# Where the third part of the hidden values is made: beside the first layer or beside the second

## The chip, the cores and the metric

The kernel runs on one core of a Trainium2 chip. The metric is the device time of one execution in microseconds (us). A core has TensorE (PE, matrix products; its weight loads are listed as PEld), VectorE (DVE), ScalarE (ACT), GpSimd (POOL) and SyncE (SP, which only starts transfers). Each engine works through its own instructions in program order and waits on semaphores for the others.

## The reference

Two blocks follow each other: a gated linear recurrence over 768 steps for 4 batches and 8 heads of 48 dimensions, and a mixture of four experts that every token goes through.

```python
for t in range(S):
    state = alpha[:, :, t, :, None] * state + np.einsum('bhd,bhe->bhde', k[:, :, t], v[:, :, t])
    y[:, :, t] = np.einsum('bhd,bhde->bhe', q[:, :, t], state)
x = y.transpose(0, 2, 1, 3).reshape(B * S, H * D)          # 3072 x 384
p = domain_probs / (domain_probs.sum(-1, keepdims=True) + 1e-09)
for e in range(E):                                         # 4 experts, F = 1024
    h = np.maximum(x @ w1[e], 0.0)
    out += p[:, e:e + 1] * (h @ w2[e])
```

All data is fp32. The change lies in the expert part alone, between `np.maximum` and `h @ w2[e]`.

## The kernel before

**Groups.** A block is 128 time steps of one batch; there are 24. They are taken in seven groups: group 0 has two blocks, groups 1 to 5 have four, group 6 has two. For each group and each expert there is a first layer (`up`, once for each of eight tiles of 128 hidden rows) and a second layer (`down`). Groups 5 and 6 alternate expert by expert at the end. While the experts of one group run, the attention of the next group's blocks is slipped in: `attention` is a generator, and `advance` runs its next stretch when a planned clock has reached the stretch's time (`deal`). The last group's attention is over before group 5 begins, so groups 5 and 6 have none beside them.

**Three parts.** TensorE multiplies most operands in a faster fp32 format[...]. To keep accuracy, operands are split in three parts that are stored one beside the other: top, low and "dif", called D here. The three products of parts (D with one part of the weights, top and low with the two others) are summed in two accumulators. From group 1 on the first layer runs in this way, from group 2 on the second layer too (`split1`, `split2`).

**First layer.** `up` takes three k-chunks of x and three parts: six products into the accumulator `one`, three into `two`, each 512 columns wide for a group of four blocks. ScalarE scales `one` into `t` (L551), VectorE adds `two` (L553). The rest, `hidden_parts`, is put off to the next tile so that it stands behind that tile's products: ScalarE makes top with a ReLU (L578), VectorE makes low (L580), and then comes D (`make_dif`, L590), one instruction for 256 columns, that is, for a pair of blocks. VectorE's order for a tile is therefore low and D of the tile before, then the add of this one.

For a group of four blocks the first 256 columns of D, those of the first pair of blocks, are made at once (L586), and the other 256 are put in the queue `later`. For group 6, with its 256 columns, all goes to `later`.

**Second layer.** `down` takes two blocks at a time (`slots`), so a group of four has a first pair and a second pair, each with 48 products of 384 columns (L624), numbered n from 0:

- 0 to 23: top, then low, of the hidden tiles 0 to 5 for both blocks
- 24 to 31: the same of tiles 6 and 7
- 32 to 39: D of tiles 0 to 7 for the pair's first block, 40 to 47 for its second block

At n = 3, 7, 11 and so on one entry is taken off `later` (L620). With eight entries, the last is made at n = 31. In a group of four blocks all eight are taken in the first pair's `down`, and they are D of the second pair.

**Sums.** A block has two accumulators in PSUM, one for top and low, one for D. When one is complete, `add_up` scales it by the expert's weight and adds it to `acc`: on VectorE (L658), but for the first expert on ScalarE where the accumulator is the first one (L656). The four PSUM buffers with the tag `g` serve `one`, `two` and the second layer's accumulators in turn, so the second pair's `down` can begin only when the first pair's first accumulator has been added up.

**Splits of x.** At the last expert of a group the next group's x is split in its three parts (`split_x`): the top parts on ScalarE at the start of the first pair, low and D on VectorE (L248, L249) in the first half of the second pair.

Of the kernel before, what the change touches and what calls it, by code (L numbers as in the profile page):

```python
# [20 lines left out]
def kernel(  # L21
# [41 lines left out]
    P = 128  # L63
# [7 lines left out]
    NT = B * P  # L71
# [11 lines left out]
    n = np.arange(QUAD)[None, :]  # L83
# [55 lines left out]
    splitting = []  # L139
    stores = deque()  # L140
    late = deque()
    later = deque()
    shared = {}
    accs = {}

# [41 lines left out]
    def load_piece(l, i, beside=False):  # L187
        if i >= E * NQ * LAST:
            return
        gi, k = divmod(i, E * NQ)  # L190
        e, c = divmod(k, NQ)
        if (split1, split2)[l](gi, e):
            w = wt[l][i] = wts.tile([P, 3, KC * QF], F32R, name=f"w{l + 1}",
                                    bufs=AHEAD if l == 0 else NQ)
            nc.sync.dma_start(out=w.bitcast(F32), in_=kept[l][k])
            return
        if l == 1 and not beside:
            return
        if l == 0:

            if gi > 0 or e == 0:
                shared[c] = wts.tile([P, 3, KC * QF], F32R, name="w2", bufs=NQ)
            w = shared[c][:, 2 - e % 2 if gi == 0 else 2].bitcast(F32)
        else:

            w = hidden[c][:, 0].rearrange("p f n -> p (f n)")[:, :KC * QF].bitcast(F32)
        wt[l][i] = w
        if l == 0:
            heads = moe_w1[e].rearrange("(h d) f -> h d f", d=D)[:, :, c * QF:(c + 1) * QF]
            w = w.rearrange("p (c f) -> p c f", f=QF)  # L210
            for part in range(2):
                nc.sync.dma_start(out=w[:, part], in_=heads[part * H // 2:(part + 1) * H // 2, :QUAD])
            nc.sync.dma_start(out=w[:, 2], in_=heads[:, QUAD:])
        else:
            nc.sync.dma_start(
                out=w.rearrange("p (c d) -> p c d", d=DM),
                in_=moe_w2[e].rearrange("(c p) d -> p c d", p=P)[:, c * FPQ:(c + 1) * FPQ])

    def split_piece(l, i):
        whole = wt[l][i]  # L220
        w = wts.tile([P, 3, KC * QF], F32R, name=f"w{l + 1}", bufs=AHEAD if l == 0 else NQ)
        top, low, dif = (w[:, part] for part in range(3))

        nc.scalar.activation(out=top, in_=whole, func=ACT.Copy, scale=TRIM)
        yield
        nc.scalar.activation(out=dif, in_=whole, func=ACT.Copy, scale=TRIM * 4096)
        yield
        nc.vector.scalar_tensor_tensor(out=low, in0=whole, scalar=4096.0, in1=dif.bitcast(F32),
                                       op0=ALU.mult, op1=ALU.subtract)
        nc.vector.tensor_sub(dif, low.bitcast(F32), top.bitcast(F32))  # L230
        nc.gpsimd.dma_start(out=kept[l][i % (E * NQ)], in_=w.bitcast(F32))
        if l == 0:
            del wt[0][i]

    def background():


        for piece in list(splitting):
            if next(piece, splitting) is splitting:
                splitting.remove(piece)  # L240
        if making and len(splitting) < 4:
            splitting.append(making.popleft())
            next(splitting[-1])
# [332 lines left out]
    def hidden_parts(x, parts):  # L576
        top, low, dif = parts
        nc.scalar.activation(out=top, in_=x, func=ACT.Relu, scale=TRIM)  # L578
        yield
        nc.vector.scalar_tensor_tensor(out=low, in0=x, scalar=0.0, in1=top.bitcast(F32),  # L580
                                       op0=ALU.max, op1=ALU.subtract)

        n = x.shape[-1]
        at = n // 2 if n == NT else 0
        if at:
            make_dif(*(part[:, :at] for part in parts))  # L586
        later.append([part[:, at:] for part in parts])

    def make_dif(top, low, dif):
        nc.vector.scalar_tensor_tensor(out=dif, in0=top.bitcast(F32), scalar=1 / 4096.0,  # L590
                                       in1=low.bitcast(F32), op0=ALU.mult, op1=ALU.subtract)
# [5 lines left out]
    def down(gi, e, slots, between):  # L597


        first = first_piece(gi, e)  # L600
        halves_ = split2(gi, e)
        if slots[0] == 0 and makes[1](gi, e):
            making.extend(split_piece(1, first + k) for k in range(NQ))
        if slots[0] == 0 and makes[0](gi, e) and 0 < e < E - 1:
            making.extend(split_piece(0, first + k) for k in range(2, NQ))
        sums = [[ps.tile([P, DM], F32, name=f"ops{j}", tag="g", bufs=4)
                 for j in range(2 if halves_ else 1)] for _ in slots]

        kinds = [((0, 1), range(FCH - 2)), ((0, 1), range(FCH - 2, FCH)), ((2,), range(FCH))]
        steps = [(part, i, fc) for parts, tiles in (kinds if halves_ else [((3,), range(FCH))])  # L610
                 for part in parts for i in range(len(slots)) for fc in tiles]
        for n, (part, i, fc) in enumerate(steps):
            c, f = divmod(fc, FPQ)
            h = hidden[c][:, :, f, slots[i] * P:(slots[i] + 1) * P]
            advance(cost(1, gi, e) / FCH / (3 if halves_ else 1))
            while between and n >= between[0][0] * len(steps):
                between.popleft()[1]()
            if n == len(steps) // 2:
                background()
            if later and n % 4 == 3:  # L620
                make_dif(*later.popleft())
            if halves_:
                w = wt[1][first + c].rearrange("p t (c d) -> p t c d", d=DM)[:, part, f]
                nc.tensor.matmul(sums[i][part // 2], lhsT=h[:, part], rhs=w,  # L624
                                 start=(fc == 0 and part != 1), stop=(fc == FCH - 1 and part != 0))
            else:
                w = wt[1][first + c].rearrange("p (c d) -> p c d", d=DM)[:, f]
                nc.tensor.matmul(sums[i][0], lhsT=h[:, 2].bitcast(F32), rhs=w,  # L628
                                 start=(fc == 0), stop=(fc == FCH - 1))
            if part >= 1 and fc == FCH - 1:  # L630
                add_up(gi, e, slots[i], part // 2, sums[i][part // 2 if halves_ else 0])
        while between:
            between.popleft()[1]()
        background()
        if slots[-1] == len(groups[gi]) - 1 and gi != LAST - 1:
            while makes[1](gi, e) and (making or splitting):
                background()

            for c in range(NQ):
                del wt[1][first + c]  # L640
                if c < NQ // 2 or gi == LAST:
                    load_piece(1, first + NQ + c)
                else:
                    late.append(first + NQ + c)

    def add_up(gi, e, slot, kind, part):

        cb, b = groups[gi][slot]
        at = b * NCB + cb
        if e == 0 and (kind == 0 or not split2(gi, e)):  # L650
            accs[cb, b] = hid.tile([P, DM], F32, name="acc", bufs=B) if gi < LAST else \
                work.tile([P, NP * P], F32, name="QT")[:, :DM]
        acc = accs[cb, b]
        scale = (p_fine if kind == 0 else p_all)[:, at, e:e + 1]
        if e == 0 and (kind == 0 or not split2(gi, e)):
            nc.scalar.activation(out=acc, in_=part, func=ACT.Copy, scale=scale)  # L656
        else:
            nc.vector.scalar_tensor_tensor(out=acc, in0=part, scalar=scale, in1=acc,  # L658
                                           op0=ALU.mult, op1=ALU.add)
        if kind == 0:  # L660
            return
        if e == E - 1:
            del accs[cb, b]
            row = b * S + cb * P
            stores.append(lambda: (nc.sync if gi >= LAST - 1 else nc.gpsimd).dma_start(
                out=out[row:row + P, :], in_=acc))
# [3 lines left out]
    def cost(layer, gi, e):  # L670
        n = len(groups[gi]) / 4
        if layer == 0:
            return 2.1 * n if split1(gi, e) else 2.6 * n
        return 4.1 if split2(gi, e) else 5.4
# [32 lines left out]
    def advance(spent):  # L707
        nonlocal clock
        clock += spent
        while waiting and clock >= waiting[0][0]:  # L710
            next(waiting.popleft()[2], None)

    with tc.manual_schedule():
# [48 lines left out]
        for (gi, e), after in zip(tasks, [*tasks[1:], (None, None)]):  # L762
# [6 lines left out]
            for k, slots in enumerate(turns):  # L769

                between = deque()
                if after[1] == 0:
                    for step, at in enumerate((0.0, 0.52, 0.62, 0.72)):
                        at = at * len(turns) - k
# [33 lines left out]
```

## Time and profile before

| | before |
|---|---|
| time, median of 3 runs | 1072.71 us (1072.09 to 1073.56) |
| span of the profiled execution | 1071.6 us |
| TensorE products busy | 1048.1 us, 98% |
| TensorE weight loads busy | 899.1 us, 84% |
| VectorE busy | 775.2 us, 72% |
| ScalarE busy | 566.7 us, 53% |
| D on VectorE (L590) | 288 instructions, 111.9 us |

The whole span is TensorE's: its products are marked busy 98% of the time. Products are pipelined and their recorded ends are modelled, so a short wait can lie under a "busy" row. The distance from one product's start to the next says more, and so does the list of what the weight loads waited for. In the rows of the timeline the first number is the start in us, the second the length of the row, then engine, line of the program, operation, what it writes and reads, shapes, and how many instructions are merged in the row; in brackets is the idle time before it and what ended it. In the lists of waits the numbers are the total in us, how many waits, and the longest. In the groups of instructions, the numbers after the count are busy us in all, mean ns of one, and idle us before them.

### The profile page before, as it was taken

To read this page: it belongs to the slowest core of one execution; us is meant where nothing else is said; L and a number is where in the kernel's file an instruction comes from. 1 tells how busy PE (TensorE), PEld (TensorE's weight loads), DVE (VectorE), ACT (ScalarE), POOL (GpSimd) and SP (SyncE) were. 2 spreads that over 40 slices of the span, in tenths; PEclk is the share of its full clock that TensorE was granted. 3 is DMA by queue.
4 is the path that set the end of the run, shared out by engine and by line. 5 is a ranking of instruction groups with operands and counts; after the bars stand their busy time and mean duration, and the time that the engine had idled before them with its cause. 6 is when DMAs were issued, how large, how long until landed. Compare 5 with 4: busy or idle time off the path is not lost.

```text
span 1071.6 us, 21614 instructions
## 1 busy us (share of the span) xinstructions
PE 1048.1 (98%) x8460; PEld 899.1 (84%) x8460; DVE 775.2 (72%) x1711; ACT 566.7 (53%) x1202; POOL 32.7 (3%) x71
## 2 busy tenths in 40 slices
PE   8899999999999999999999999999999999999998
PEld 8777777676776798898898898898889889898988
DVE  5488776656566978778877777986787866666565
ACT  5687866575656554536546445555464543323232
POOL 2010000000000100000000000000000000000000
PEclk9999999999999999999999999999999999999999
DMA  8597699687696967758759558586594543544540
GB/s 123 156 330 216 230 328 368 238 328 241 236 309 209 402 216 274 281 160 312 268 170 359 204 187 337 186 281 234 158 358 173 221 192 147 207 177 178 187 181 31
DMA packets 158838, 251.67 MB, mean 235 GB/s; under 512 B 120112, under 2 KB 135344, under 8 KB 136208
## 3 DMA queue, kind: packets, MB, share of 16 engines
q1 hardware_dynamic: 149600, 208.82, 57.1%
q0 software_dynamic: 5760, 41.29, 9.8%
q8 instruction: 67, 1.10, 0.4%
q10 hardware_dynamic: 3376, 0.17, 0.3%
q14 instruction: 35, 0.29, 0.1%
HBM read 207.79 MB, written 42.47 MB: 234 GB/s over the span
## 4 chain that ended last, share of the span: by engine, by line
PE 83%; DVE 8%; ACT 6%; issue 2%; DMA 1%; SPq 0%; DVEq 0%; ACTq 0%
PE ops L624 25%; PE one L540 21%; PE ops L628 10%; PE two L540 10%; PE sc L334 6%; PE yps L428 3%; PE tp L266 3%; PE one L532 2%; ACT qb L308 2%; PE far L389 1%; PE sps L463 1%; DVE near L344 1%; DVE t L553 1%; DVE hT L580 1%; DVE hT L590 1%
## 5 line engine op out<-in xcount | busy, mean ns | idle before, releaser
L624 PE MATMUL ops<-w,hT 128*128 128x384 f32 x1728 | 318.0, 339 | 4.4 <-DVE acc L658 4.3
L624 PEld LDWEIGHTS ops<-w,hT 128*128 128x128 f32 x1728 | 299.1, 188 | 9.9 <-DVE acc L658 5.6
L540 PE MATMUL one<-xT,w 128*128 128x512 f32 x960 | 253.8, 400 | 2.6 <-DVE xT L248 1.1
L540 PEld LDWEIGHTS one<-xT,w 128*128 128x128 f32 x960 | 176.3, 188 | 41.8 <-DVE QT L315 1.6
L551 ACT ACTIVATE t<-one 128x512 f32<-128x512 f32 (+1 forms) x192 | 106.3, 554 | 153.6 <-PE one L540 148.5
L308 ACT COPY qb<-QT 64x256 f32<-64x256 f32 x336 | 136.4, 406 | 77.0 <-DVE QT L289 44.1
L578 ACT ACTIVATE hT<-t 128x512 fp32r<-128x512 f32 (+1 forms) x160 | 94.3, 589 | 123.6 <-DVE t L553 122.9
L580 DVE SCALAR_TENSOR_TENSOR hT<-t,hT 128x512 fp32r<-128x512 f32 (+1 forms) x160 | 102.2, 638 | 55.7 <-ACT hT L578 53.6
L540 PE MATMUL two<-xT,w 128*128 128x512 f32 x480 | 136.7, 393 | 0.0
L628 PE MATMUL ops<-hT 128*128 128x384 f32 x384 | 133.4, 491 | 0.0
L553 DVE TENSOR_TENSOR t<-t,two 128x512 f32<-128x512 f32 (+1 forms) x160 | 100.8, 630 | 41.9 <-ACT t L551 21.4
L590 DVE SCALAR_TENSOR_TENSOR hT<-hT 128x256 fp32r<-128x256 f32 x288 | 111.9, 422 | 4.4
L540 PEld LDWEIGHTS two<-xT,w 128*128 128x128 f32 x480 | 90.6, 189 | 20.0
L628 PEld LDWEIGHTS ops<-hT 128*128 128x128 f32 x384 | 69.5, 190 | 40.1 <-issue 0.4
L315 DVE TENSOR_TENSOR QT<-QT,dec 128x256 f32<-128x256 f32 x144 | 60.8, 422 | 38.2 <-ACT qb L308 37.5
L344 DVE COPY_PREDICATED near<-masks,sc 128x256 f32<-128x256 uint8 x144 | 77.0, 535 | 15.5 <-PE sc L334 12.8
L334 PEld LDWEIGHTS sc<-qb,KT 128*64 128x64 f32 x2304 | 72.7, 138 | 9.7 <-issue 5.6
L334 PE MATMUL sc<-qb,KT 128*64 128x64 f32 x2304 | 77.2, 223 | 2.6 <-ACT qb L308 2.6
L658 DVE SCALAR_TENSOR_TENSOR acc<-ops,p_all,acc 128x384 f32<-128x384 f32 x82 | 49.5, 614 | 33.9 <-PE ops L624 14.5
L326 ACT COPY KT<-KT 128x256 f32<-128x256 f32 x144 | 59.9, 416 | 3.2
L327 DVE TENSOR_TENSOR KT<-KT,dec 128x256 f32<-128x256 f32 x144 | 60.3, 419 | 0.0
L558 DVE TENSOR_TENSOR hT<-t,two 128x512 f32<-128x512 f32 x32 | 22.0, 688 | 35.6 <-ACT t L551 23.0
(88 smaller groups left out, 970.7 us busy)
## 6 DMA issues: line engine op xcount, KB each, us to landing
w<-kept SPq DMA_DIRECT2D x144, 1152.0 KB
kept<-w POOLq DMA_DIRECT2D x32, 1152.0 KB, 7.4
hT<-in_moe_w_dram SPq DMA_DIRECT2D x32, 384.0 KB
w<-in_moe_w_dram SPq DMA_DIRECT2D x48, 128.0 KB
ra<-in_alpha_dram SPq DMA_DIRECT2D x23, 192.0 KB
rk<-in_k_dram SPq DMA_DIRECT2D x23, 192.0 KB
rq<-in_q_dram SPq DMA_DIRECT2D x23, 192.0 KB
out_dram<-acc POOLq DMA_DIRECT2D x18, 192.0 KB, 6.6
```

What stands on the lines that cost most here:

```text
L308: nc.scalar.copy(out=qb[rows, :, i, :].rearrange("p a (b r) -> p a b r", r=m), in_=qv[rows])
L315: nc.vector.tensor_mul(qv, qv, spread(dv[:, :, :, 0], m))
L334: nc.tensor.matmul(out[HALF * s:HALF * (s + 1), 2 * p:2 * p + 2, :], lhsT=KTs[li][:, p, HALF * s:HALF * (s + 1)], rhs=qbs[li][:, p, :, QUA ...
L344: nc.vector.copy_predicated(near.rearrange("p a (b two r) -> p a b two r", two=2, r=m)[:, :, :, 1, :], mk.unsqueeze(1).broadcast_to([P, H, ...
L540: nc.tensor.matmul(out, lhsT=w[:, part, kc], rhs=x_part(gi, part, kc), start=(part == terms[0] and kc == 0), stop=(part == terms[-1] and k ...
L551: nc.scalar.activation(out=t, in_=one, func=ACT.Copy, scale=FINE)
L553: nc.vector.tensor_add(t, t, two)
L578: nc.scalar.activation(out=top, in_=x, func=ACT.Relu, scale=TRIM)
L580: nc.vector.scalar_tensor_tensor(out=low, in0=x, scalar=0.0, in1=top.bitcast(F32), op0=ALU.max, op1=ALU.subtract)
L590: nc.vector.scalar_tensor_tensor(out=dif, in0=top.bitcast(F32), scalar=1 / 4096.0, in1=low.bitcast(F32), op0=ALU.mult, op1=ALU.subtract)
L624: nc.tensor.matmul(sums[i][part // 2], lhsT=h[:, part], rhs=w, start=(fc == 0 and part != 1), stop=(fc == FCH - 1 and part != 0))
L628: nc.tensor.matmul(sums[i][0], lhsT=h[:, 2].bitcast(F32), rhs=w, start=(fc == 0), stop=(fc == FCH - 1))
```

## The change

D of the first pair is no longer made in the first layer. All of D is put in two queues, one for each pair of blocks, and a pair's `down` takes from its own queue, one piece of 256 columns at each fourth product. So the first pair's D is made while the first pair's top and low products run, and the second pair's D while the second pair's run. The change is meant to take VectorE work out of the first layer, where VectorE has most to do, and to spread it over both halves of the second. Group 6, with one pair, keeps what it had. The arithmetic and the order of TensorE's products are the same.

```diff
-    later = deque()
+    later = [deque(), deque()]
...
-        n = x.shape[-1]
-        at = n // 2 if n == NT else 0
-        if at:
-            make_dif(*(part[:, :at] for part in parts))
-        later.append([part[:, at:] for part in parts])
+        for k in range(0, x.shape[-1], 2 * P):
+            later[k // (2 * P)].append([part[:, k:k + 2 * P] for part in parts])
...
-            if later and n % 4 == 3:
-                make_dif(*later.popleft())
+            dif = later[slots[0] // 2]
+            if dif and n % 4 == 3:
+                make_dif(*dif.popleft())
```

## The prediction

> **What bounds the kernel now.** I read the page first (engine shares, then the costliest groups), then the list of waits of TensorE's weight loads, then the timeline of one pair of layers on TensorE and VectorE side by side.
>
> ```profile
> PE 1048.1 (98%) x8460; PEld 899.1 (84%) x8460; DVE 775.2 (72%) x1711; ACT 566.7 (53%) x1202; POOL 32.7 (3%) x71
> L590 DVE SCALAR_TENSOR_TENSOR hT<-hT 128x256 fp32r<-128x256 f32 x288 | 111.9, 422 | 4.4
> PEld ops L624 <- DVE acc L658: 5.6, 4, 2.2
> PEld ops L624 <- ACT t L551: 1.4, 7, 0.3
> PEld ops L624 <- DVE t L553: 1.3, 4, 0.4
> ```
>
> The first line says TensorE is fed nearly all the time, so a change on VectorE can only win back TensorE's few waits. The next is the operation that the change moves. The last three are TensorE's waits in the second layer that VectorE or ScalarE causes: 5.6 us in four places (the second pair of blocks waits until an accumulator of the first pair has been added up) and 2.7 us of crumbs. One of the four, in group 3, expert 1, in two timelines:
>
> ```profile
> 582.32 0.85 PE L540 MATMUL two<-xT,w 128*128 128x512 f32 x3
> 583.00 0.51 PE L624 MATMUL ops<-w,hT 128*128 128x384 f32 x2
> 583.71 3.90 PE L624 MATMUL ops<-w,hT 128*128 128x384 f32 x21
> 587.79 3.72 PE L624 MATMUL ops<-w,hT 128*128 128x384 f32 x20
> 591.71 1.12 PE L624 MATMUL ops<-w,hT 128*128 128x384 f32 x5
> 593.30 0.97 PE L624 MATMUL ops<-w,hT 128*128 128x384 f32 x4 [0.48 <-DVE acc L658]
> ```
>
> ```profile
> 578.25 0.69 DVE L553 TENSOR_TENSOR t<-t,two 128x512 f32<-128x512 f32 x1 [0.71 <-ACT t L551]
> 580.36 0.42 DVE L590 SCALAR_TENSOR_TENSOR hT<-hT 128x256 fp32r<-128x256 f32 x1
> 585.17 0.42 DVE L590 SCALAR_TENSOR_TENSOR hT<-hT 128x256 fp32r<-128x256 f32 x1
> 587.01 0.69 DVE L580 SCALAR_TENSOR_TENSOR hT<-t,hT 128x512 fp32r<-128x512 f32 x1 [0.70 <-ACT hT L578]
> 587.74 0.42 DVE L590 SCALAR_TENSOR_TENSOR hT<-hT 128x256 fp32r<-128x256 f32 x1
> 588.83 1.76 DVE L590 SCALAR_TENSOR_TENSOR hT<-hT 128x256 fp32r<-128x256 f32 x5
> 591.97 0.75 DVE L590 SCALAR_TENSOR_TENSOR hT<-hT 128x256 fp32r<-128x256 f32 x2
> 592.63 0.61 DVE L658 SCALAR_TENSOR_TENSOR acc<-ops,p_fine,acc 128x384 f32<-128x384 f32 x1
> 593.16 0.42 DVE L590 SCALAR_TENSOR_TENSOR hT<-hT 128x256 fp32r<-128x256 f32 x1
> ```
>
> The first pair's 48 products run from 583.00 to 592.7. VectorE trails: the last tile's low part (L580) comes at 587.01, four us after TensorE has left the first layer, and the eight pieces of D for the second pair follow from 588.83 to 593.58. Nobody waits for those eight yet, for the second pair reads its D only in its own last third. Just before the eighth stands the add (592.63) that lets TensorE go on at 593.30.
>
> [...] the "busy" rows above cover small waits, so I went by distances between starts, 174 ns for a 384-column product here. [...] The trace has 422 and 682 to 693; but back to back a piece takes (1.76-0.42)/4 = 0.335 us, and that is what I use. [...] a late VectorE instruction stops all of TensorE's products behind the one that needs it.
>
> **The change part by part.** The count of pieces stays 288 and so does VectorE's total. In the 16 layer pairs of groups 2 to 5, eight pieces (the first pair's D) leave the first layer and go into the first pair's second layer, at its products 3, 7, ... 31; the eight of the second pair move on into the second pair's products. Group 6 keeps its order. No product, transfer or ScalarE instruction moves.
>
> What it takes away: VectorE's lag at the end of the first layer. The four waits of 5.6 us should go, as the add for block 0 then comes earlier, and most of the crumbs: about 1.4 of 2.7 us. In all 7.0 us.
>
> What it adds: the first pair's last third starts at product 32, one piece per product for block 0, so the piece of tile 7 is due at product 39. Before, it had been made in the first layer. Now it stands where the second pair's eighth piece stood. In the example product 39 starts at 587.79 + 0.09 + 16 x 0.174 = 590.66 (the row of 20 begins with product 23), and that place in VectorE's queue is over at 593.58: 2.92 us late. How much earlier does the queue get there? Work that the change can't advance is the add at 578.25, which waited for ScalarE and so for TensorE. Behind it only three removed pieces stand (580.36, 585.17, 587.74), 3 x 0.35 = 1.05 us. TensorE waits 2.92 - 1.05 = 1.87 us, where it waited 0.6 before.
>
> The same reading in the other layer pairs, lateness of that eighth place minus what is won behind the last fixed point (a wait for a product, for the state update's products or for scores). Group 2: 1.51-1.44 = 0.07, 2.71-1.38 = 1.33, nothing, 1.56-0.79 = 0.77. Group 3: 1.53-0.68 = 0.85, 1.87, 2.74-1.15 = 1.59, 2.50-1.84 = 0.66. Group 4: 2.52-1.57 = 0.95, 3.93-2.35 = 1.58, nothing, 3.46-0.70 = 2.76. Group 5 has no attention beside it; its VectorE lag is drift alone (starts of L553 are 2.45 us apart against 2.07 us of products, and without the piece 2.1), so all eight pieces count, 2.8 us against 1.63 late: nothing. Sum 12.4 us.
>
> The second pair: there VectorE has 1.4 to 4.7 us idle up to product 32 in most layer pairs, which holds eight pieces (2.7 us) together with what was won before. Not at the last expert of groups 2, 3 and 4, where the six splits of the next group's x (L248, L249, some 4 us) fall in the same stretch and idle is 0.14 to 0.27 us. Seven pieces ahead of the add add 2.35 us, less the advance carried over, and the eighth follows at once. In group 3 that add ran at 686.97: 686.97 - 1.84 + 2.35 - 0.14 = 687.34, the piece is done 0.87 later at 688.2, and product 39, at 686.13 now and about as early then, waits 2.1. Group 2 gives 0.9 in the same way and group 4 0.1. Sum 3.1 us.
>
> The waits themselves: a product that finds its piece made costs nothing. Group 6 already makes its D in this way, and its products stand 174 ns apart through the last third.
>
> Sum: 12.4 + 3.1 - 7.0 = +8.5 us, so 1072.7 + 8.5 = 1081.2 us.
>
> **The rivals.** A, the forecast above: late pieces replace the add's wait. B, faster: VectorE uses the relief fully. If all eight pieces' 2.8 us were won in each layer pair, lateness would shrink to 0.1 + 1.1 + 0.7 = 1.9 us, the second pairs' waits to about 1, and 7.0 would be won: -4, about 1068.5. For it speaks that VectorE is idle 2 to 4 us in each first layer; against it that this idle time is spent waiting for TensorE and ScalarE (L580 on L578: 53.6 us in all), before the last attention piece, and can't be stored up. C, a wash: twice my advance (about 1.2 more in each of the ten late places) leaves some 3 us in first pairs and 3 in second, against 7: about 1072. D, worse: the advance is lost because attention work and adds in the queue then wait for TensorE instead. With none of it the first pairs wait 25 us and group 5 another 5; with a third lost, 12.4 + 4 and the second pairs 3.1 + 2: some 1087.
>
> **How the numbers follow.** A 0.60, D 0.18, C 0.12, B 0.10. The predicted time is A's, 1081.2. The range goes from 1073.5 (just above C, most of the mass of A's milder forms) to 1088 (D with the cost of one lost third); below it lie B and half of C. Faster by over 0.2% (under 1070.6): 0.11, B and a little of C. Within: 0.10. Slower (over 1074.9): 0.79.
>
> **What would show it.** Right: the wait of the second layer on L658 gone, and in its place TensorE waits in front of the second layer for L590 (the line that makes D), ten or more places of 0.6 to 2.8 us in groups 2 to 4, none in group 5, the longest with the last expert of group 4, and one of 2 us in the second pair of group 3's last expert. The first layer shows L553 closer to 2.1 us apart. Wrong: no waits on L590 above a few us in all, which would mean VectorE gets ahead by more than I allow; or waits in group 5, which would mean that the piece itself or its place in the queue costs more than the gap of four products.

## The result and the profile after

The changed kernel takes 1087.29 us (median of 4 runs, 1085.77 to 1088.04) where the kernel before takes 1073.13 in the runs beside it. The ratio is 1.0131, with a 95% interval from 1.0113 to 1.0149: 14 us slower.

The page of the changed kernel, with the engine shares and the two groups that tell the story (line numbers after the diff are two or three smaller: the second layer's product is L622, D is L587, the add is L656):

```profile
PE 1054.6 (97%) x8460; PEld 899.7 (83%) x8460; DVE 771.9 (71%) x1711; ACT 569.3 (52%) x1202; POOL 32.8 (3%) x71
...
L622 PEld LDWEIGHTS ops<-w,hT 128*128 128x128 f32 x1728 | 299.4, 188 | 23.3 <-DVE hT L587 18.2
...
L587 DVE SCALAR_TENSOR_TENSOR hT<-hT 128x256 fp32r<-128x256 f32 x288 | 105.3, 419 | 0.0
```

And its list of what the weight loads waited for (us in total, times, longest), the lines for the second layer:

```profile
PEld ops L622 <- DVE hT L587: 18.2, 25, 2.0
...
PEld ops L622 <- ACT t L551: 0.6, 4, 0.2
```

The waits for the add, 5.6 us before, are gone. In their place stand 25 waits for D, 18.2 us, the longest 2.0. The number of D's instructions is the same, and VectorE as a whole does no more than before. Only their places have changed.

The same pair of blocks as in the prediction, group 3, expert 1, first pair. TensorE:

```profile
586.72 0.51 PE L622 MATMUL ops<-w,hT 128*128 128x384 f32 x2
...
587.42 3.89 PE L622 MATMUL ops<-w,hT 128*128 128x384 f32 x21
...
591.51 2.68 PE L622 MATMUL ops<-w,hT 128*128 128x384 f32 x14
594.99 0.78 PE L622 MATMUL ops<-w,hT 128*128 128x384 f32 x2 [0.80 <-DVE hT L587]
596.19 0.97 PE L622 MATMUL ops<-w,hT 128*128 128x384 f32 x4 [0.42 <-DVE hT L587]
```

VectorE:

```profile
589.91 0.69 DVE L580 SCALAR_TENSOR_TENSOR hT<-t,hT 128x512 fp32r<-128x512 f32 x1 [0.70 <-ACT hT L578]
...
591.38 1.76 DVE L587 SCALAR_TENSOR_TENSOR hT<-hT 128x256 fp32r<-128x256 f32 x5
593.06 0.42 DVE L315 TENSOR_TENSOR QT<-QT,dec 128x256 f32<-128x256 f32 x1
593.39 0.15 DVE L317 TENSOR_TENSOR dec<-dec 128x4 f32<-128x4 f32 x1
593.47 0.55 DVE L285 TENSOR_TENSOR t<-rq,rk 128x384 f32<-128x384 f32 x1
594.05 0.55 DVE L286 TENSOR_REDUCE dot<-t 128x8 f32<-128x384 f32 x1
594.52 0.75 DVE L587 SCALAR_TENSOR_TENSOR hT<-hT 128x256 fp32r<-128x256 f32 x2
595.19 0.61 DVE L656 SCALAR_TENSOR_TENSOR acc<-ops,p_fine,acc 128x384 f32<-128x384 f32 x1
595.72 0.41 DVE L587 SCALAR_TENSOR_TENSOR hT<-hT 128x256 fp32r<-128x256 f32 x1
```

Read from the bottom: the eighth piece comes at 595.72, and the product that needs it, number 39, starts at 596.19. Right ahead of the piece stands an add (595.19), and ahead of the sixth and seventh a stretch of the next group's attention (593.06 to 594.5). From 591.38 on VectorE has no idle time. It does what it must, in an order that puts the urgent piece last. Counted from the pair's first product, the piece comes after 9.0 us, against 10.2 for that place before, so 1.2 us were won in the first layer. It was due after 7.7.

Where the time went can be had without the modelled ends of rows. In the second layer of groups 2 to 6 the products start 174 ns apart when nothing holds them (in groups 0 and 1, where this layer's operands are plain fp32, the trace of before has 384 instructions for 192 products of this width at L628, and they start 323 ns apart). The table sums what the distances have over that, for each place where it is more than 40 ns (100 where other products lie between), in five parts of a layer pair. "D, first pair" is products 31 to 45.

| kernel | start, first pair | D, first pair | on to the second pair | second pair, before D | D, second pair | after it | sum | time |
|---|---|---|---|---|---|---|---|---|
| before | 3.5 | 0.9 | 5.0 | 1.9 | 0.2 | 0.0 | 11.4 | 1073.1 |
| changed | 1.9 | 15.0 | 0.0 | 1.5 | 6.9 | 0.2 | 25.5 | 1087.3 |

The sums are of one profiled execution each. The sum grows by 14.1 us and the median time by 14.2, so the loss lies in these places. Nearly all of it is waits for D; about 0.7 us in the second pairs' 6.9 is a granted TensorE clock of 0.50, shown further down.

### The profile page after: what moved, and what is told of

Its sections match the earlier page's. It is cut to its first block, busy times and chain, and to the rows that moved or that the text cites. A ratio compares the mean times of both kernels' runs of the same rounds, so it can differ in the third digit from the quotient of the medians.

```text
span 1085.3 us, 21589 instructions
## 1 busy us (share of the span) xinstructions
PE 1054.6 (97%) x8460; PEld 899.7 (83%) x8460; DVE 771.9 (71%) x1711; ACT 569.3 (52%) x1202; POOL 32.8 (3%) x71
## 4 chain that ended last, share of the span: by engine, by line
PE 76%; DVE 12%; ACT 7%; issue 2%; DMA 2%; SPq 0%; DVEq 0%; ACTq 0%
PE ops L622 21%; PE one L540 20%; PE ops L626 10%; PE two L540 10%; PE sc L334 5%; PE yps L428 3%; DVE hT L587 2%; PE tp L266 2%; PE one L532 2%; ACT qb L308 2%; DVE near L344 2%; DVE t L553 2%; DVE QT L315 1%; PE far L389 1%; ACT hT L578 1%
## 5 line engine op out<-in xcount | busy, mean ns | idle before, releaser
L622 PE MATMUL ops<-w,hT 128*128 128x384 f32 x1728 | 324.4, 342 | 11.8 <-DVE hT L587 11.7
L622 PEld LDWEIGHTS ops<-w,hT 128*128 128x128 f32 x1728 | 299.4, 188 | 23.3 <-DVE hT L587 18.2
L587 DVE SCALAR_TENSOR_TENSOR hT<-hT 128x256 fp32r<-128x256 f32 x288 | 105.3, 419 | 0.0
L656 DVE SCALAR_TENSOR_TENSOR acc<-ops,p_all,acc 128x384 f32<-128x384 f32 x82 | 50.2, 616 | 31.9 <-PE ops L622 13.7
```

## The experiments

Three accounts stood against each other. The place: TensorE waits because a piece of D stands in VectorE's queue behind work that isn't due, so moving it helps although the load is the same. The load: the second layer's halves hold more VectorE work than they have time for. The waits: a product that must look for its own piece costs something even when the piece is there.

**The same load, other places.** Only the first pair's D is moved into its products; the second pair's is made in the first layer. In each stretch VectorE then has exactly as many pieces as before the change. The edits of this section are against the changed kernel, but for the last one.

```diff
-        for k in range(0, x.shape[-1], 2 * P):
-            later[k // (2 * P)].append([part[:, k:k + 2 * P] for part in parts])
+        n = x.shape[-1]
+        if n == NT:
+            make_dif(*(part[:, 2 * P:] for part in parts))
+        later[0].append([part[:, :2 * P] for part in parts])
```

> Only the first pair's D is moved, into the first pair's products; the second pair's is made in the first layer at once. Every stretch then holds exactly as many pieces as in the kernel before. Place: nothing is won in the first layer, so the first pairs wait for the whole lateness of the eighth place as the trace of before shows it, 23.4 us in groups 2 to 4 and about 6 in group 5, less the 5.6 of the add: about 1097 us, 1091 to 1101. Load: the same load in each stretch, so 1073. Waits: half the waiting products of the changed kernel, about 1080.

Measured 1106.18 us, ratio 1.0299 (1.0283 to 1.0314). The load can't explain 33 us, since it is that of before. The direction is the place's, but the size is off by 9: first pairs lose 37.1 us, not 29. Three things make up most of the 9. The latenesses that the prediction lists for groups 2 to 4 add up to 25.4, with 2.92 for its example, and not to the 23.4 that was used here. In expert 2 of groups 2 and 4, where nothing was expected, the first pairs lose about 1 us each. About 5 us, an estimate worked out further down, come from stretches with a granted TensorE clock of 0.50. The other latenesses hold: in the eight pairs of groups 2 to 4 that have one and that the slower clock doesn't touch, this run's loss is within 0.2 us of the one listed.

**The other half of the change.** The first pair's D stays in the first layer, the second pair's goes into the second pair's products.

```diff
-        for k in range(0, x.shape[-1], 2 * P):
-            later[k // (2 * P)].append([part[:, k:k + 2 * P] for part in parts])
+        n = x.shape[-1]
+        if n == NT:
+            make_dif(*(part[:, :2 * P] for part in parts))
+            later[1].append([part[:, 2 * P:] for part in parts])
+        else:
+            later[0].append(parts)
```

> Only the second pair's D is moved, into the second pair's products; the first pair's is made in the first layer, as in the kernel before. Place: no first pair waits for D, the add's four waits of 5.6 us go since the eight pieces no longer stand before the add, and the second pairs of three or four layer pairs wait some 4 us in all: 1071 us, 1069 to 1074. Load: the first layer is as full as before and the second pair's half as full as in the changed kernel, so 1078 or more. Waits: half the waiting products of the changed kernel, about 1080.

Measured 1077.15, ratio 1.0036 (1.0024 to 1.0049). A miss for the place by 3 us, and nearer to the load. The first pairs do lose nothing on D (0.9 us as before), but the second pairs lose 8.2 on D where I had 4 (about 1 of it, an estimate, is a granted clock of 0.50), and one of the add's waits stays, 1.7 us in group 4, expert 1. So for the second pairs the load was still open after this run.

**The other half, with the pieces placed sooner.** The same kernel with a piece per two products:

```diff
-            if dif and n % 4 == 3:
+            if dif and (n % 2 == 1 if gi < LAST else n % 4 == 3):
```

> First pair's D in the first layer as before, only the second pair's moved, but with a piece per two products. Theory of the place: the second pairs' waits that the same move with a piece per four products had, 8.2 us, go down to about 0.5: 1069.5 us, 1068 to 1072. Theory of the load, which the 1077 of that run agreed with: the first layer and the second pair's half hold as much VectorE work as there, so 1076 to 1078.

Measured 1069.91, ratio 0.9966 (0.9953 to 0.9978). Second pairs lose 0.5 us on D with the same pieces in the same half. So the place was the cause there too: the eighth piece at product 15 and not at 31.

**The change itself, with other paces.** The condition of the diff alone is altered, for three, two and one products per piece; group 6 keeps four.

```diff
-            if dif and n % 4 == 3:
+            if dif and (n % 3 == 2 if gi < LAST else n % 4 == 3):
```

> The changed kernel with a piece per three products in the groups of four blocks, so that the last of eight is placed at product 23 and not at 31. Theory of the place: the last piece is then ahead of the adds of products 29 and 31 and of the attention slipped in after product 23; the second pairs' waits of 6.9 us shrink to about 2 and the first pairs' 15 to about 8: 1076 us, 1072 to 1080. If the gain from four to two products has one threshold, the two adds alone, then it is all there already: 1070 to 1072.

```diff
-            if dif and n % 4 == 3:
+            if dif and (n % 2 == 1 if gi < LAST else n % 4 == 3):
```

> Theory of the place (mine): TensorE waits because the piece of tile 7 stands in VectorE's queue behind the adds of product 29 and a stretch of attention, eight products before it is due. With a piece per two products all eight stand ahead of these, so most waits of the second layer on D go: about 1072 us, 1069 to 1076, where the changed kernel has 1087. Theory of the load: the halves of the second layer hold more VectorE work than they have time for, wherever the pieces stand: 1085 to 1089. Theory of the waits: each product that has to look for its own piece costs something even when the piece is there: 1085 to 1089 too.

```diff
-            if dif and n % 4 == 3:
+            if dif and (gi < LAST or n % 4 == 3):
```

> A piece per product, all eight placed in the first eight products of their pair. Theory of the place: the first pairs' waits left with a piece per two products, 4.5 us in the trace, shrink to 1 to 2, since only attention slipped in before product 8 is still ahead: 1068 us, 1066 to 1070. Rival: what is left comes from the last tile's low part being late, or the attention pushed back by eight pieces in a row makes new waits elsewhere: 1070 to 1074.

Measured 1075.95 (ratio 1.0026, 1.0017 to 1.0036), 1070.48 (0.9966, 0.9953 to 0.9979) and 1068.72 (0.9954, 0.9939 to 0.9969). With four it was 1087.29. These four kernels have the same instructions, the same number of pieces in each pair and about as many weight loads of the second layer that wait on VectorE (362 with four products per piece, 374 with fewer); only the places differ, and the time falls at every step. This rules out the load and the cost of satisfied waits, and it rules out one threshold at the two adds, for from three to two products 5 us more are won. The last kernel is faster than both kernels of this case.

The same two timelines of group 3, expert 1, first pair, with a piece per product. VectorE:

```profile
584.80 0.69 DVE L580 SCALAR_TENSOR_TENSOR hT<-t,hT 128x512 fp32r<-128x512 f32 x1 [0.70 <-ACT hT L578]
...
586.27 2.77 DVE L587 SCALAR_TENSOR_TENSOR hT<-hT 128x256 fp32r<-128x256 f32 x8
588.95 0.42 DVE L315 TENSOR_TENSOR QT<-QT,dec 128x256 f32<-128x256 f32 x1
```

TensorE:

```profile
582.31 3.89 PE L622 MATMUL ops<-w,hT 128*128 128x384 f32 x21
...
586.40 3.72 PE L622 MATMUL ops<-w,hT 128*128 128x384 f32 x20
...
590.31 1.81 PE L622 MATMUL ops<-w,hT 128*128 128x384 f32 x9
```

All eight pieces run in one go soon after the low part of the last tile and end at 589.04, ahead of the next stretch of attention and of the adds. The row of 20 products, which holds number 39, runs through without a stop.

**Only the second pair's pieces, behind the adds.** The first pair's D stays in the first layer. The other eight are placed at products 35 to 47 of the first pair and 3 to 15 of the second. The edit is against the kernel before; not shown is the new queue `single`, which takes group 6's pieces.

```diff
-            if later and n % 4 == 3:
-                make_dif(*later.popleft())
+            dif = later if later and (slots[0] or n >= 2 * len(steps) // 3) else single
+            if dif and n % 4 == 3:
+                make_dif(*dif.popleft())
```

> As before the change, but the second pair's eight pieces stand later: at products 35, 39, 43 and 47 of the first pair and 3, 7, 11 and 15 of the second, so behind the adds of the first pair's first accumulators and well ahead of their use. Place: the add's four waits of 5.6 us go and nothing takes their place: 1067.5 us, 1066 to 1070. Load: the second pair's half gets four pieces more, at the last experts where it is full: 1073 to 1076. Waits: 1073, as no product waits more often than before.

Measured 1071.24, ratio 0.9974 (0.9963 to 0.9985). A gain, but less than I had said, and outside the 1066 to 1070 of the expectation: three of the four waits for the add go, the one of group 4, expert 1, stays with 1.7 us, and 1.1 us are new after the second pair of group 3's last expert.

All kernels in the parts of the first table:

| kernel | start, first pair | D, first pair | on to the second pair | second pair, before D | D, second pair | after it | sum | time |
|---|---|---|---|---|---|---|---|---|
| first pair's D alone moved | 3.4 | 37.1 | 0.6 | 3.2 | 0.2 | 0.0 | 44.5 | 1106.2 |
| second pair's alone, per four | 3.2 | 0.9 | 1.7 | 1.6 | 8.2 | 0.2 | 15.8 | 1077.2 |
| second pair's alone, per two | 3.5 | 0.9 | 1.7 | 1.6 | 0.5 | 1.1 | 9.3 | 1069.9 |
| changed, per three | 1.9 | 8.7 | 0.3 | 1.5 | 3.8 | 0.0 | 16.2 | 1076.0 |
| changed, per two | 1.9 | 4.5 | 0.0 | 1.5 | 0.2 | 1.1 | 9.3 | 1070.5 |
| changed, per one | 1.9 | 2.8 | 0.4 | 1.6 | 0.2 | 1.2 | 8.1 | 1068.7 |
| second pair's behind the adds | 3.5 | 0.9 | 1.7 | 1.6 | 0.5 | 1.1 | 9.2 | 1071.2 |

Times follow the sums to within 2.5 us. Of the rest, 1.2 to 1.7 us lie ahead of group 2, where no D is made and all kernels are alike; the section on the hardware has the reason.

## Why the prediction was right, and what it missized

The forecast was slower, 1081.2 us; it is 1087.3, inside the range and by the likeliest case's mechanism: late pieces of D take the place of the add's waits. The size was not as good: 8.5 us were forecast and 14.2 came. That the time still lies in the range is in part luck, since the range reached 1088 for the sake of rival D, whose lost advance did not come.

What it takes away, 7.0 us: right. The add's waits fall from 5.0 to 0 in the table, the start of the first pair from 3.5 to 1.9, the second pair's from 1.9 to 1.5, which is 7.0.

What is won ahead of the pieces: right in the example. In group 3, expert 1, I had 1.05 us and a wait of 1.87; the trace has 1.2 and 1.9. The run that gives this advance up, by making the second pair's D in the first layer, loses 37.1 us in the first pairs against 15.0, the slower clock included.

First pairs, 12.4 us: measured 14.1, the 15.0 of the table less the 0.9 that before had. All layer pairs but two are within 0.2 us; the first two experts of group 4 wait 1.7 and 2.1 where I had 0.95 and 1.58. For the first of them the run without the advance shows a lateness of 2.7, near the 2.52 that I had, so it was the advance that I put too high, at 1.57 where about 1.0 was won; why is not shown.

Group 5, nothing: right. Its pairs show no waits for D, and from its start to the end the changed kernel wins 1.0 us (it begins 14.8 us later and ends 13.8 later).

Second pairs, 3.1 us: the term that was missized. The table has 6.9, and 0.7 more falls into the next first layer. I had said that idle time up to product 32 holds the eight pieces except at the last experts. In group 4, expert 1, VectorE does have idle time, but ahead of product 29; the eighth piece stands behind the add that waits for that product, and a stretch of attention is slipped in between the two:

```profile
786.17 0.62 DVE L656 SCALAR_TENSOR_TENSOR acc<-ops,p_fine,acc 128x384 f32<-128x384 f32 x1 [1.46 <-PE ops L622]
786.70 0.42 DVE L315 TENSOR_TENSOR QT<-QT,dec 128x256 f32<-128x256 f32 x1
787.03 0.17 DVE L317 TENSOR_TENSOR dec<-dec 128x16 f32<-128x16 f32 x1
787.12 0.42 DVE L327 TENSOR_TENSOR KT<-KT,dec 128x256 f32<-128x256 f32 x1
787.45 0.89 DVE L344 COPY_PREDICATED near<-masks,sc 128x256 f32<-128x256 uint8 x2
788.25 0.42 DVE L587 SCALAR_TENSOR_TENSOR hT<-hT 128x256 fp32r<-128x256 f32 x1
```

VectorE sits idle for 1.46 us ahead of the add, and the piece, which is behind the add in the queue, starts only 2.1 us after the add does: those 1.46 us were not spent on it. This one place costs 1.3 us, and with a piece per three products, at 23, it costs nothing. The largest share is group 3's last expert: I had 2.1 us, and it loses 3.3 and the 0.7. There the wait for the seventh and eighth piece is 2.7 us, which is near, and the rest is the clock.

What would show it wrong, waits in group 5 or only a few us on D, didn't come. Rival B had less room than its 0.10: in the trace only the pieces behind the last fixed point counted. D, with a third of the advance lost, gave 1087, the measured time, but by another way: but for about 1.2 us in group 4 the advance was there, and the second pairs, the clock with them, made up the sum.

## What the runs showed of the hardware

After some clusters of short waits the granted clock of TensorE was 0.50 for 3.4 or 6.8 us. The second pair of group 3's last expert in the changed kernel, TensorE's timeline and then the busy times by stretch (after the stretch: its length, then busy us of each engine, the granted clock as a share of full speed, the DMA share and GB/s):

```profile
687.40 4.78 PE L622 MATMUL ops<-w,hT 128*128 128x384 f32 x26
693.84 0.77 PE L622 MATMUL ops<-w,hT 128*128 128x384 f32 x2 [1.66 <-DVE hT L587]
695.03 2.73 PE L622 MATMUL ops<-w,hT 128*128 128x384 f32 x9 [0.42 <-DVE hT L587]
697.55 1.80 PE L540 MATMUL one<-xT,w 128*128 128x512 f32 x4
```

```profile
693.00:695.00 2.00, 0.77 (x2) 0.37 (x2) 2.00 (x6) 0.97 (x2) 0.00 (x0) 1.00 0.01 4
695.00:697.00 2.00, 1.97 (x8) 1.97 (x9) 1.90 (x5) 0.00 (x0) 0.00 (x0) 0.67 0.26 32
697.00:699.00 2.00, 2.00 (x7) 1.72 (x6) 0.62 (x1) 0.00 (x0) 0.83 (x2) 0.50 0.69 272
699.00:701.00 2.00, 2.00 (x10) 1.65 (x9) 0.37 (x1) 1.11 (x3) 0.25 (x1) 0.98 1.02 396
```

From 695 on nothing is late any more, and yet nine products take 2.5 us, the later ones starting 0.32 apart instead of 0.17, and the first layer's 0.43 apart instead of 0.23. The granted clock is 0.50 from 695.7 to 699.1, 3.4 us. By the distances of starts that costs 1.6 us, 0.9 in the second layer and 0.7 in the first. A stretch of 3.4 us at 0.50 also follows the waits of group 3's last expert with the second pair's D alone moved, a piece per four (from 687.65), and those of group 4's last with the changed kernel's two queues and a piece per three (from 851.9). In the kernel with only the first pair's D moved it happens in two stretches of 6.8 us each; the first, from the busy times by stretch:

```profile
784.00:786.00 2.00, 1.83 (x6) 1.63 (x6) 1.75 (x4) 0.00 (x0) 0.00 (x0) 0.50 0.00 0
786.00:788.00 2.00, 2.00 (x8) 2.00 (x7) 0.66 (x2) 0.00 (x0) 0.00 (x0) 0.50 0.00 0
788.00:790.00 2.00, 2.00 (x10) 2.00 (x10) 1.04 (x4) 0.00 (x0) 0.00 (x0) 0.77 0.00 0
```

For part of these stretches TensorE waits for D in any case. The products that start 0.32 us apart instead of 0.17, counted one by one, come to about 5 us (an estimate), over half of the 9 by which the expectation fell short.

In the changed kernel's trace the two stretches at 0.50 that end within it begin at 166.62 and 695.68 and are 3.413 us long each; their starts lie 155 times that length apart. In the kernel with only the first pair's D moved, the other trace with more than one, they begin at 167.71, 782.11 and 874.27, 180 and 27 times that length apart. None of the waits ahead of the stretch at 695.68 was that long: the longest was 1.8 us (by the distances of starts), and six products started in the 3.4 us before it. A few waits close together stood there, but such a cluster isn't always followed by the slow clock: in the same kernel the waits of 0.4, 0.9 and 0.7 us between 860 and 864.3 left the granted clock at 1.00. What sets off such a stretch, these runs don't show. The busy share doesn't show it either: from 697 to 699 in the changed kernel TensorE is busy for 2.00 of 2.00 us at a granted clock of 0.50.

Not every such stretch belongs to the change. The profile of the kernel before has one of 3.4 us at 0.50 from 167.4, ahead of group 2; so have those of the changed kernel, of the one with only the first pair's D moved and of the one with a piece per two products. The profiles of the other five don't, and from about 170 us on they are 1.2 to 1.7 us ahead of it, with the same products. So of the 4.7 us that a piece per product wins, about 3.3, the difference of the sums, belong to the places.

## What to carry to other kernels

When work is moved to "just beside" its use, write down for each piece the product that needs it and everything that stands ahead of it in its engine's queue at that place, adds that wait and work that is slipped in included; the load of the stretch tells nothing of that. Here the same eight instructions per pair cost 14 us at one piece per four products and won 4.7 at one per product, of which about 3.3 are owed to the places. Count idle time of the engine only if it lies behind the last wait ahead of the piece: here 1.46 us of it ahead of an add did nothing for the piece behind that add. And look at the granted clock after a cluster of waits on TensorE: in the changed kernel 3.4 us at 0.50 followed one and cost 1.6 us on top of the waits.
